# Eight buffers in place of six for one product, and a plan fitted to them: attention recurrence and gated MLP on one core

## The chip, the cores and the metric

The kernel runs on one core of a Trainium2 chip. Its engines are TensorE (PE, with its weight loads listed as PEld), VectorE (DVE), ScalarE (ACT), GpSimd (POOL) and SyncE (SP), which here issues all transfers. Each engine takes its instructions strictly in the order of the program. The metric is the device time of one execution in microseconds.

## The reference

A recurrent attention runs over 768 steps for 4 batches of 8 heads with head size 40, and its output goes through an MLP without an activation function:

```python
for t in range(S):
    y[:, :, t] = np.einsum('bhd,bhde->bhe', rt, state)
    Sa = np.einsum('bhde,bhe->bhd', state, at)
    state_decay = state * wt[:, :, None, :] - np.einsum('bhd,bhe->bhde', Sa, bt)
    state = state_decay + np.einsum('bhd,bhe->bhde', vt, kt)
...
x = np.ascontiguousarray(attn_out.transpose(0, 2, 1, 3)).reshape(B * S, H * D)
a = x @ w1
b = x @ w2
h = a * b @ w3
return (h @ w_out).astype(np.float32)
```

The MLP has 3072 tokens, 320 inputs and 1024 hidden columns. Its weights arrive as 64-bit numbers.

## The kernel before, in words

The 768 steps are cut into 12 chunks of 64. In a chunk the recurrence is a product with a triangular system, so that only 12 steps are sequential. A chunk is worked in four groups (g = 0 to 3, one for each batch, of four head pairs each). Its parts, with their lines:

- **load**: SP brings fm (decays and the k and b factors, L425) and al (a, L428).
- **scale**: DVE forms the running product of the decays (L438, L443), ACT its inverse (L447, L450), DVE refines that (L459, L463). lh is a times the decay (L455, POOL), and fm's second part is scaled by the inverse (L467).
- **causal**: PE multiplies lh with fm (L492). ACT copies parts of the result to JP and, negated, back into lh (both listed as L205), where POOL cuts the triangle (L510).
- **solve**: once a chunk, after the causal products of all four groups, DVE transposes JP (L524) and inverts the small triangular blocks in some fifty rows (L550, L554 and others up to L599 and L602). There is one buffer for this, ab.
- **join**: PE joins the inverted blocks (L625, L632), ACT copies them to TT.
- **pairs, tokens**: products that don't need the state (L669, L679, L694).
- **rec**: the recurrence of one group. PE reads the state (L719), multiplies with lh (L726), applies the solved blocks (L735); DVE masks the result (L740, four rows for a group); PE adds it up (L748); DVE forms the new state and the output y (L772, L792), PE transposes the state (L779). After L726 the group's lh is free, after L792 its fm.
- **gather, mlp**: SP moves y to xr (L802), ACT and DVE split it into two parts (L827, L830), PE multiplies (L844), ACT and DVE form the product of the two halves (L858, L861), PE multiplies by the product of w3 and w_out (L870), SP stores (L879).

In the head the weights are converted from 64 bits (L317 to L341) and split (L383, L395), and w3 is multiplied with w_out (L405). No MLP can begin before that.

What sets the order is a planner inside the kernel. Every operation is recorded with an engine, a cost, a due time, what it reads and writes, and the buffers it holds. `place()` then goes through a list schedule with these costs: on each engine the operation that can start first comes next, and among several the one with the earliest due time. A buffer of a pool is taken at the first operation that uses it and is given back after the last. The instructions are issued in that order, so the costs and the due times decide the program's order and nothing at run time. Numbers of buffers stand in `SLOTS`, distances of due times from a chunk's time in `P` (chunk time T0 + T x chunk), and `ON` says for some operations whether DVE or POOL does them in which chunk. lh is one pool of 6 buffers in the order of use, fm has 8, al 4.

Of the kernel before, what the change touches and what calls it, by code (L numbers as in the profile page):

```python
# [14 lines left out]
ALU = mybir.AluOpType  # L15
# [13 lines left out]
WMAX, GMIN = 1.5, 2.0 ** -40  # L29
CW = 512  # L30
LAT = dict(pe=0.33, act=0.09, dve=0.09, pool=0.1, sp=2.4, nil=0.0)
SLOTS = dict(rc=2, fm=8, al=4, lh=6, gi=2, gt=1, ab=1, TDX=1, rv=3, xu=3, bk=3, hs=2, st=2, y=1, xr=1, JP=2, TT=2, bank=6,
             raw=4, e=3, sg=3, mf=4, w3f=3, xs=1, gh=1, gl=1, ga=2, o=2)


ENGINES = tuple(getattr(mybir.EngineType, n) for n in ("PE", "Activation", "DVE", "Pool", "SP"))
T0, T = 32.93, 43.48
P = dict(w0=12.33, ws=3.58, ld=71.12, sc=40.48, ca=45.61, so=6.14, sp=45.27, jo=3.14, pa=8.34, tk=5.31, rg=14.14,
         ga=6.52, ml=90.63, kp=1.61, mt=25.46, mg=10.0)

ON = dict(cv="ppdpppdppppdddppppdpppppdddpppp", ws="d", lh="pppppppppppp", xs="dppppppppppp", gl="ppppppppppdd",
          cb="dddddddddddddddddddpdpddddddppp")


class Slot:


    def __init__(self, order, pool):
        self.order, self.pool, self.at, self.left, self.since, self.until = order, pool, None, 0, 0.0, 0.0
        if order.direct:  # L50
            self.at = order.turn[pool] = (order.turn.get(pool, -1) + 1) % SLOTS[pool]

# [5 lines left out]
class Order:  # L58
# [33 lines left out]
    def place(self):  # L92
# [3 lines left out]
        for o in ops:  # L96
            for d in o["deps"]:
                ops[d]["users"].append(o)
        free = {p: dict.fromkeys(range(n), 0.0) for p, n in SLOTS.items()}
        ready = {e: [] for e in LAT}  # L100
# [20 lines left out]

        uses = {p: {o["eng"] for o in ops for s in o["slots"] if s.pool == p} for p in SLOTS}
        placed, cand, spare = [], {}, {}

        def choice(e, starts):
            if not starts:
                return None
            first = min(t for t, _ in starts)
            return first, min((o for t, o in starts if t <= first + 1e-9),
                              key=lambda o: (o["due"] - P["kp"] * (e == "pe" and o["kind"] == last), o["n"]))  # L130

        while len(placed) < len(ops):
            best = None
            for e in LAT:
                if e not in cand:

                    starts, short = [], 1e9
                    for o in ready[e]:
# [3 lines left out]
                        elif e == "pe" and any(s.pool == "bank" and s.at is None for s in o["slots"]):  # L142
                            short = min(short, o["due"] + P["mg"])
                    some = [x for x in starts if x[1]["due"] < short or not any(s.at is None for s in x[1]["slots"])]
# [49 lines left out]
def attention_moe(ctx: ExitStack, tc: tile.TileContext, fmx, fma, rv, vt, sq, svr, w12, w12c, w3t, wo, out):  # L194
    nc = tc.nc
    pe, act, dve, pool = nc.tensor, nc.scalar, nc.vector, nc.gpsimd
    sp = nc.sync
# [10 lines left out]
    ident = cp.tile([128, 128], F32, name="ident")  # L208
# [3 lines left out]
    for q in range(2):  # L212
# [5 lines left out]
    pool.memset(first[:, :, 0:1], 1.0)  # L218
    parity = cp.tile([128, 1], F32, name="parity")

    dve.tensor_reduce(out=parity, in_=ident.rearrange("p (a b c) -> p a b c", a=4, b=2)[:, :, 1, :],
                      axis=mybir.AxisListType.XY, op=ALU.add)

    DG = cp.tile([128, 4, 8, 8], F32, name="DG")
    pool.memset(DG, 0.0)
# [11 lines left out]


    SB = cp.tile([104, NPC // 2, 2, 64], F32, name="SB")
    dve.memset(SB, 0.0)  # L240
    W3 = [cp.tile([128, NJ, DM], F32R, name=f"W3{n}") for n in "hl"]
    WT = [None] * 5
    for i in (0, 2):
# [4 lines left out]
    tiles = {}  # L248
    for name, shape in dict(fm=[104, 772], al=[104, NP, C], lh=[128, 2, NP, C], gi=[104, NP, C], gt=[104, NP, C], 
                            TDX=[128, 1024], rv=[104, 2, 2, 2 * C + D], xu=[128, 2, NP, C + D], bk=[128, NP, 104],  # L250
                            hs=[128, NP, C + D], st=[104, NP, D], y=[104, NP, TOK], xr=[128, 3, TOK],
                            JP=[128, NPC, 2, 32], TT=[128, NPC, C]).items():
        pl = cp if name == "TT" else ap_
        tiles[name] = [pl.tile(shape, F32, name=f"{name}{i}") for i in range(SLOTS[name])]
    for t in tiles["TT"]:
        dve.memset(t, 0.0)
    for t in tiles["al"]:
        dve.memset(t[32:64], 0.0)
    for t in tiles["rv"]:
        for h in range(2):  # L260
            q = slice(64 * h, 64 * h + 40)
            pool.tensor_copy(out=t[q].rearrange("q u x n -> q (u x) n")[:, :, 2 * C:],
                             in_=ident[q, q].unsqueeze(1).to_broadcast([40, 4, D]))
    tmp = ap_.tile([128, 1024], F32, name="tmp")
    R8 = ap_.tile([128, 8, 8], F32, name="R8")
    tiles["ab"] = [ps.tile([128, 1024], F32, name="ab")]
    tiles["bank"] = [ps.tile([128, 512], F32, name=f"bank{i}") for i in range(SLOTS["bank"])]


    cv, pp = ExitStack(), ExitStack()  # L270
    cvp = cv.enter_context(tc.tile_pool(name="cv", bufs=1, side="right"))
    for name, n, dt in (("raw", CW, I64), ("e", CW, U16), ("sg", CW, BF16), ("mf", CW, F32)):
        tiles[name] = [cvp.tile([128, n], dt, name=f"{name}{i}") for i in range(SLOTS[name])]
    ppp = pp.enter_context(tc.tile_pool(name="pp", bufs=1))
# [17 lines left out]
    op, slot = order.op, order.slot  # L292
# [16 lines left out]
    def convert(src, dst, due, w=()):  # L309
# [38 lines left out]
        op("dve", 0.62, due, f6, r=[raw], w=[mf], two=True)  # L348
        both(ON["cb"][k], 1.2, 0.38, due, f7, r=[e], w=[sg])
        both(ON["cv"][k], 1.25, 0.62, due, f8, r=[sg, "conv"], w=[mf] if dst is None else [mf, *w])  # L350
        return mf

    def weights():

        due, step = P["w0"], P["ws"]
        for k in range(3):
# [576 lines left out]
    for c in range(NCH):  # L933
        t0 = T0 + T * c
        jp_[c], tt_[c], y_[c] = slot("JP"), slot("TT"), slot("y")
        for g in range(B):
            load(c, g, t0 - P["ld"] + 2 * g)
        for g in range(B):
            scale(c, g, t0 - P["sc"] + 3 * g)
            causal(c, g, t0 - P["ca"] + 3 * g)  # L940
        solve(c, t0 - P["so"], P["sp"])
# [105 lines left out]
```

## Time and profile before

| what | us |
|---|---|
| median of three runs | 756.51 |
| the profiled execution, its own time | 756.74 |
| span of the profiled execution | 755.0 |
| busy PE, DVE, ACT, POOL | 608.8, 579.6, 480.3, 290.7 |
| first L844 (MLP) | 212.4 |
| last L870 ends | 749.1 |

The rows of the timeline have the start, the duration, the engine, the line and the operation, output and input, and in brackets the idle time before it with what ended it. In the rows of waits stand the waiting instruction, what it waited for, the sum, the number of times and the longest. In groups by line stand the busy time, the mean in ns, and the idle time before. Where a line's matmuls are listed, an f32 product counts two instructions.

### The profile page before, as it was taken

Reading aid. Unit: us, or ns where it says so; the run is one execution under the profiler, and the core shown is the slowest. Engines: PE = TensorE matmul, PEld = TensorE weight load, DVE = VectorE, ACT = ScalarE, POOL = GpSimd, SP = SyncE. Lnnn points to the kernel's source line nnn. Section 1 sums busy time; section 2 is a strip of 40 time slices with the busy share of each in tenths; the row PEclk is TensorE's granted clock in tenths of the full one; section 3 lists DMA queues with packets and bytes.
Section 4 is the critical chain, followed back from the end, with each engine's and each line's share of the span. In section 5 each row is a group of like instructions: output and inputs, shape, how many; then the busy total and the mean of one; then the engine's idle time right before and its main releaser. Section 6 shows DMA issues by size and latency. Waiting matters only on the chain.

```text
span 755.0 us, 23802 instructions
## 1 busy us (share of the span) xinstructions
PE 608.8 (81%) x9458; PEld 525.1 (70%) x9458; DVE 579.6 (77%) x1317; ACT 480.3 (64%) x1309; POOL 290.7 (39%) x374
## 2 busy tenths in 40 slices
PE   1312199658689899898898998998989989999996
PEld 1211176336579788797787887977878779788996
DVE  6969999899885895985968959859589498693421
ACT  3744466458857668768676687686767776836431
POOL 3155414534443363443533634435426244321000
PEclk9999999877779999999999999999999999999999
DMA  7833264134220312313113233142232231211010
GB/s 181 223 90 96 81 184 143 44 123 135 62 51 15 97 51 70 88 44 98 50 51 96 50 74 83 46 97 53 54 89 57 63 80 46 55 28 44 8 35 20
DMA packets 67554, 57.63 MB, mean 76 GB/s; under 512 B 31600, under 2 KB 58480, under 8 KB 67440
## 3 DMA queue, kind: packets, MB, share of 16 engines
q1 hardware_dynamic: 67440, 56.08, 27.9%
q8 instruction: 76, 1.25, 0.7%
q14 instruction: 38, 0.31, 0.1%
HBM read 47.40 MB, written 3.93 MB: 68 GB/s over the span
## 4 chain that ended last, share of the span: by engine, by line
DVE 31%; PE 21%; ACT 18%; issue 6%; SPq 3%; DMA 1%; POOL 0%; DVEq 0%; ACTq 0%; POOLq 0%
PE bank L844 8%; DVE tmp L550 6%; ACT JP L205 5%; ACT TT L205 4%; DVE xu L740 3%; PE bank L870 3%; PE bank L748 3%; SPq L802 3%; PE bank L492 2%; DVE ab L524 2%; DVE DG L554 2%; ACT xu L205 2%; DVE fm L443 2%; DVE ga L858 2%; DVE Tp L554 2%
## 5 line engine op out<-in xcount | busy, mean ns | idle before, releaser
L844 PE MATMUL bank<-xs,W 128*128 128x256 f32 x1536 | 205.5, 288 | 2.3 <-issue 1.7
L844 PEld LDWEIGHTS bank<-xs,W 128*128 128x128 f32 x1536 | 188.4, 190 | 10.3 <-issue 3.7
L740 DVE TENSOR_TENSOR xu<-bank,mask_h 64x208 f32<-64x208 f32 x192 | 71.2, 371 | 57.7 <-PE bank L735 54.5
L467 POOL TENSOR_TENSOR fm<-fm,gi 104x512 f32<-104x512 f32 x44 | 62.7, 1425 | 117.0 <-DVE gi L463 91.2
L205 ACT ACTIVATE xu<-bank 64x128 f32<-64x128 f32 (+2 forms) x368 | 90.7, 297 | 19.0 <-PE bank L669 9.2
L205 ACT ACTIVATE JP<-bank 32x256 f32<-32x256 f32 (+1 forms) x216 | 75.7, 350 | 38.2 <-PE bank L492 34.8
L510 POOL TENSOR_SCALAR_AFFINE_SELECT lh<-lh 64x256 f32<-64x256 f32 x96 | 39.9, 415 | 129.6 <-ACT lh L205 125.8
L455 POOL TENSOR_TENSOR lh<-al,fm 104x512 f32<-104x512 f32 x48 | 59.5, 1245 | 43.5 <-PE bank L726 32.5
L748 PE MATMUL bank<-xu,bk 128*40 128x104 f32 (+1 forms) x768 | 49.6, 262 | 24.2 <-DVE xu L740 24.2
L726 PE MATMUL bank<-xu,lh 104*64 104x104 f32 (+2 forms) x768 | 53.2, 272 | 17.4 <-ACT xu L205 9.1
L861 POOL TENSOR_TENSOR gl<-ga,gh 128x512 fp32r<-128x512 f32 x40 | 51.5, 1286 | 32.8 <-ACT gh L205 32.8
L679 POOL TENSOR_SCALAR_AFFINE_SELECT xu<-xu 64x256 f32<-64x256 f32 x96 | 41.2, 429 | 57.7 <-ACT xu L205 49.6
L870 PE MATMUL bank<-W3h,gh 128*128 128x320 f32 x192 | 63.2, 329 | 0.0
L748 PEld LDWEIGHTS bank<-xu,bk 128*40 128x40 f32 (+1 forms) x768 | 37.4, 118 | 34.0 <-DVE xu L740 29.0
L726 PEld LDWEIGHTS bank<-xu,lh 128*64 128x64 f32 (+2 forms) x768 | 41.4, 145 | 27.9 <-ACT xu L205 16.5
L870 PE MATMUL bank<-W3l,gh 128*128 128x320 f32 x192 | 59.3, 309 | 0.0
L870 PE MATMUL bank<-W3h,gl 128*128 128x320 f32 x192 | 59.1, 308 | 0.0
L205 ACT ACTIVATE gh<-ga 128x512 fp32r<-128x512 f32 x48 | 30.1, 628 | 38.1 <-DVE ga L858 37.8
L447 ACT ACTIVATE gi<-fm 104x256 f32<-104x256 f32 x48 | 20.0, 416 | 53.7 <-DVE fm L443 51.2
L694 PE MATMUL bank<-ident,fm 104*128 104x104 f32 x192 | 28.8, 277 | 29.9 <-DMA al<-in_fma_dram 11.6
L405 PE MATMUL bank<-wof,w3f 128*128 128x320 f32 x128 | 44.2, 497 | 6.4 <-POOL w3f L341 6.2
L492 PE MATMUL bank<-lh,fm 40*64 40x64 f32 x1536 | 38.8, 238 | 12.8 <-POOL fm L467 8.3
(102 smaller groups left out, 1297.5 us busy)
## 6 DMA issues: line engine op xcount, KB each, us to landing
fm<-in_fmx_dram SPq DMA_DIRECT2D x48, 313.6 KB
raw<-in_w3t_dram SPq DMA_DIRECT2D x16, 512.0 KB
rv<-in_rv_dram SPq DMA_DIRECT2D x96, 80.0 KB
raw<-in_w_dram SPq DMA_DIRECT2D x8, 512.0 KB
al<-in_fma_dram SPq DMA_DIRECT2D x96, 40.0 KB
xu<-in_vt_dram SPq DMA_DIRECT2D x96, 40.0 KB
out_dram<-o SPq DMA_DIRECT2D x48, 80.0 KB
xr<-y SPq DMA_DIRECT2D x72, 40.0 KB
```

Of the source, the lines that this page charges most:

```text
L205: act.activation(out_, in_, AF.Copy, scale=scale)
L405: pe.matmul(out=pt.t[:, 0:DM], lhsT=w[:, j], rhs=wof[:, j], start=(j == 0), stop=(j == NJ - 1))
L455: e.tensor_tensor(out=lh.t[0:104], in0=al.t.unsqueeze(1).to_broadcast(full), in1=gam(c, g)[:, :, 0:C].unsqueeze(1).to_broadcast(full), op= ...
L467: e.tensor_tensor(out=X, in0=X, in1=gi.t.unsqueeze(2).to_broadcast([104, NP, 2, C]), op=ALU.mult)
L492: pe.matmul(out=bank(ab)[64 * x:64 * x + 64, p], lhsT=X[r, p, x], rhs=lh.t[r, ab, p], start=True, stop=True)
L550: dve.tensor_tensor(out=scratch(*shape), in0=x().to_broadcast([128, *shape]), in1=y().to_broadcast([128, *shape]), op=ALU.mult)
L726: pe.matmul(out=view(hp)[64 * ab:64 * ab + 64, p], lhsT=lh.t[k, ab, p], rhs=xu.t[k, ab, p], start=True, stop=True)
L740: dve.tensor_tensor(out=xu.t[64 * ab:64 * ab + 64, ab, k:NP:2], in0=qs[ab].t[r, 256:256 + 2 * N].rearrange("p (n t) -> p n t", n=2), in1=m ...
L748: pe.matmul(out=q(r, p), lhsT=bk.t[:, p, r], rhs=xu.t[:, ab, p], start=(c == 0), stop=True, skip_group_check=True)
L844: pe.matmul(out=pt.t[:, TOK * x:TOK * x + TOK], lhsT=WT[k][:, cs], rhs=xs.t[:, z], start=(n == 0), stop=(n == 7))
L861: both(ON["gl"][c % NCH], 1.35, 0.62, t + 1, lambda e, a=a, j=j: e.tensor_tensor(out=gl.t[:, j:j + 2], in0=a.t, in1=gh.t[:, j:j + 2], op=A ...
L870: pe.matmul(out=pt.t[:, 0:DM], lhsT=l.t[:, j, ts], rhs=W3[r][:, j], start=(j == 0 and n == 0), stop=(j == NJ - 1 and n == 2))
```

## The change

lh gets eight buffers, al three. The numbers in `P` are new, and with them the due times. In `ON` a few operations change between DVE and POOL: L467 of chunk 8 goes to DVE, L861 of chunks 7 and 10 to DVE and that of chunk 11 to POOL, two L338 to DVE and one L341 to POOL. At the start the memsets change their order, al first.

```diff
-SLOTS = dict(rc=2, fm=8, al=4, lh=6, gi=2, gt=1, ab=1, TDX=1, rv=3, xu=3, bk=3, hs=2, st=2, y=1, xr=1, JP=2, TT=2, bank=6,
+SLOTS = dict(rc=2, fm=8, al=3, lh=8, gi=2, gt=1, ab=1, TDX=1, rv=3, xu=3, bk=3, hs=2, st=2, y=1, xr=1, JP=2, TT=2, bank=6,
...
-P = dict(w0=12.33, ws=3.58, ld=71.12, sc=40.48, ca=45.61, so=6.14, sp=45.27, jo=3.14, pa=8.34, tk=5.31, rg=14.14,
-         ga=6.52, ml=90.63, kp=1.61, mt=25.46, mg=10.0)
-
-ON = dict(cv="ppdpppdppppdddppppdpppppdddpppp", ws="d", lh="pppppppppppp", xs="dppppppppppp", gl="ppppppppppdd",
-          cb="dddddddddddddddddddpdpddddddppp")
+P = dict(w0=13.15, ws=3.46, ld=92.51, sc=40.41, ca=51.28, so=6.14, sp=36.96, jo=5.76, pa=9.53, tk=2.89, rg=10.82,
+         ga=5.8, ml=85.76, kp=3.48, mt=30.46, mg=11.62)
+
+ON = dict(cv="ppdpppdppppdddppppdpppppddppppp", ws="d", lh="pppppppppppp", xs="dpppppppdppp", gl="pppppppdppdp",
+          cb="dddddddddddddddddddpdpddddddddp")
...
-    dve.tensor_reduce(out=parity, in_=ident.rearrange("p (a b c) -> p a b c", a=4, b=2)[:, :, 1, :],
-                      axis=mybir.AxisListType.XY, op=ALU.add)
...
-    dve.memset(SB, 0.0)
...
-    for t in tiles["TT"]:
-        dve.memset(t, 0.0)
-    for t in tiles["al"]:
-        dve.memset(t[32:64], 0.0)
...
+    for t in tiles["al"]:
+        dve.memset(t[32:64], 0.0)
+    dve.memset(SB, 0.0)
+    for t in tiles["TT"]:
+        dve.memset(t, 0.0)
+    dve.tensor_reduce(out=parity, in_=ident.rearrange("p (a b c) -> p a b c", a=4, b=2)[:, :, 1, :],
+                      axis=mybir.AxisListType.XY, op=ALU.add)
```

Most of what the change does is in the order that the planner makes of this. Three places of it follow.

DVE, from the end of a chunk's solve (L602) on, before. Names: TDX the solved blocks, xs the MLP's input, fm the decays, xu the masked rows:

```order
L602 STREAM_TRANSPOSE TDX_117<-TDX_117 128x512
L830 TENSOR_TENSOR xs_1852<-xr_132,xs_1852 128x768
L438 TENSOR_SCALAR fm_103,stats<-fm_103 104x260
L443 SCALAR_TENSOR_TENSOR fm_103<-fm_103,first 104x260
L459 TENSOR_TENSOR gt_116<-fm_103,gi_115 104x256
L463 SCALAR_TENSOR_TENSOR gi_115<-gt_116,gi_115 104x256
L740 TENSOR_TENSOR xu_122<-bank_154,mask_h 64x2x104
```

The same place now, in every second chunk of the repeating part:

```order
L602 STREAM_TRANSPOSE TDX_116<-TDX_116 128x512
L443 SCALAR_TENSOR_TENSOR fm_101<-fm_101,first 104x260
L459 TENSOR_TENSOR gt_115<-fm_101,gi_114 104x256
L463 SCALAR_TENSOR_TENSOR gi_114<-gt_115,gi_114 104x256
L858 TENSOR_TENSOR ga_1864<-bank_153,ga_1864 128x512
L524 STREAM_TRANSPOSE ab<-JP_133 128x1024
L550 TENSOR_TENSOR tmp<-DG,ab 128x4
L554 TENSOR_REDUCE DG<-tmp 128x4
L550 TENSOR_TENSOR tmp<-DG,ab 128x16
```

The next chunk's solve (L524) now begins ahead of this chunk's masks (L740); thirteen solve rows of L550 and L554 and one L830 stand between L524 and the masks. Before, L524 stood behind the masks and outputs of two groups. In the other chunks it now follows the masks of the first group.

DVE, from a group's output to the next use of the same fm buffer, before:

```order
L792 TENSOR_TENSOR y_131<-bank_153,fm_98 104x2x64
L792 TENSOR_TENSOR y_131<-bank_157,fm_98 104x2x64
L554 TENSOR_REDUCE ab<-tmp 128x8x4
L858 TENSOR_TENSOR ga_1853<-bank_155,ga_1853 128x512
L459 TENSOR_TENSOR gt_116<-fm_97,gi_115 104x256
L463 SCALAR_TENSOR_TENSOR gi_115<-gt_116,gi_115 104x256
L550 TENSOR_TENSOR tmp<-Tp,ab 128x256
```

There follow three more solve rows and four masks, and then L438 of fm_98. The shortest such stretch now:

```order
L792 TENSOR_TENSOR y_130<-bank_157,fm_97 104x2x64
L792 TENSOR_TENSOR y_130<-bank_154,fm_97 104x2x64
L594 TENSOR_TENSOR ab<-R_150,ab 128x8x8
L550 TENSOR_TENSOR tmp<-ab,DG 128x512
L554 TENSOR_REDUCE Tp<-tmp 128x8x8
L599 STREAM_TRANSPOSE TDX_116<-Tp 128x32x16
L602 STREAM_TRANSPOSE TDX_116<-TDX_116 128x512
L438 TENSOR_SCALAR fm_97,stats<-fm_97 104x260
```

Between giving the buffer back and wanting it filled again stand five rows of DVE; the load lies between them, on SP.

PE, between the recurrences of two groups, from the sum (L748) of the first group of a chunk on. lh is read by L726. Now:

```order
L748 MATMUL bank_153<-xu_121,bk_124 40x104 x4
L748 MATMUL bank_154<-xu_121,bk_124 40x104 x4
L726 MATMUL bank_155<-xu_122,lh_106 64x104 x8
L694 MATMUL bank_156<-ident,fm_97 128x104 x4
L779 MATMUL bank_153<-ident,st_128 40x104 x4
L844 MATMUL bank_154<-xs_1862,W_0_91 128x256 x2
```

Before, the same place reads:

```order
L735 MATMUL bank_154<-hs_128,TT_136 64x104
L735 MATMUL bank_152<-hs_128,TT_136 64x104
L748 MATMUL bank_153<-xu_121,bk_124 40x104 x4
L748 MATMUL bank_157<-xu_121,bk_124 40x104 x4
L694 MATMUL bank_155<-ident,fm_103 128x104 x4
```

Before, the first two groups of a chunk went together, L735 of both ahead of L748 of the first. Now in the repeating part the first group's L748 comes before the second group's L735, with MLP rows (L870, L844) between them.

## The prediction, as put on record

> **What bounds the kernel now.** I read the page first, then the windows, then the timeline of one repeating stretch, engine by engine.
>
> ```profile
> span 755.0 us, 23802 instructions
> PE 608.8 (81%) x9458; PEld 525.1 (70%) x9458; DVE 579.6 (77%) x1317; ACT 480.3 (64%) x1309; POOL 290.7 (39%) x374
> PE   1312199658689899898898998998989989999996
> DVE  6969999899885895985968959859589498693421
> ```
>
> The rows by slices show two regimes: a head of some eleven slices in which DVE is full and PE is not, and a body in which PE is at 8 or 9 of 10 and DVE swings. The windows (columns: PE, PEld, DVE, ACT, POOL busy us, then clock and DMA) put numbers on them.
>
> ```profile
> 0.00:213.50 213.50, 108.69 (x1469) 80.38 (x1469) 190.13 (x393) 124.45 (x312) 87.10 (x116) 0.91 0.42 121
> 245.50:295.40 49.90, 46.03 (x786) 40.25 (x784) 39.49 (x96) 36.22 (x104) 22.48 (x29) 1.00 0.27 70
> 497.30:547.20 49.90, 46.09 (x785) 40.36 (x786) 39.47 (x96) 36.21 (x104) 22.02 (x29) 1.00 0.28 70
> 693.50:755.00 61.50, 55.00 (x568) 52.21 (x566) 20.44 (x44) 17.45 (x38) 0.82 (x2) 0.99 0.09 23
> ```
>
> The body repeats chunk by chunk. Its first and last chunk begin (first L735 of chunk 2 and of chunk 11) at:
>
> ```profile
> 245.49 0.59 PE L735 MATMUL bank<-hs,TT 64*64 64x104 f32 x16
> 693.46 1.27 PE L735 MATMUL bank<-hs,TT 64*64 64x104 f32 x32
> ```
>
> That is nine intervals of (693.46 - 245.49)/9 = 49.8 us. No engine is full in them: PE is busy 46.1, DVE 39.5. So a cycle of waits sets the interval. DVE's timeline shows it:
>
> ```profile
> 497.28 3.12 DVE L740 TENSOR_TENSOR xu<-bank,mask_h 64x208 f32<-64x208 f32 x8 [5.00 <-PE bank L735]
> 503.21 1.98 DVE L524 STREAM_TRANSPOSE ab<-JP 128x1024 f32<-128x1024 f32 x1 [1.31 <-ACT JP L205]
> 512.72 1.53 DVE L740 TENSOR_TENSOR xu<-bank,mask_h 64x208 f32<-64x208 f32 x4
> 520.26 1.53 DVE L740 TENSOR_TENSOR xu<-bank,mask_h 64x208 f32<-64x208 f32 x4
> 530.24 0.68 DVE L550 TENSOR_TENSOR tmp<-ab,DG 128x512 f32<-128x512 f32 x1
> 536.48 0.71 DVE L602 STREAM_TRANSPOSE TDX<-TDX 128x512 f32<-128x512 f32 x1
> 541.28 0.42 DVE L459 TENSOR_TENSOR gt<-fm,gi 104x256 f32<-104x256 f32 x1 [2.17 <-ACT gi L450]
> 547.23 1.95 DVE L740 TENSOR_TENSOR xu<-bank,mask_h 64x208 f32<-64x208 f32 x5 [5.00 <-PE bank L735]
> ```
>
> DVE masks two head groups (L740), starts the solve (L524), works without a pause to the solve's end (L602 ends at 537.2), and then has next to nothing until PE has joined the blocks and reached the next chunk's L735: a handoff of 10.0 us (537.2 to 547.2), idle in 7.2 of it. With the 1.31 before L524 that is 8.5 idle, so DVE is occupied 49.9 - 8.5 = 41.4 us a chunk. PE's side of the same stretch:
>
> ```profile
> 510.23 2.15 PE L844 MATMUL bank<-xs,W 128*128 128x256 f32 x16
> 513.91 1.13 PE L748 MATMUL bank<-xu,bk 128*40 128x104 f32 x16 [1.52 <-DVE xu L740]
> 514.97 1.21 PE L844 MATMUL bank<-xs,W 128*128 128x256 f32 x8
> 516.71 0.54 PE L779 MATMUL bank<-ident,st 104*40 104x104 f32 x4 [0.53 <-DVE y L792]
> 525.32 6.83 PE L844 MATMUL bank<-xs,W 128*128 128x256 f32 x56
> 537.46 1.20 PE L625 MATMUL bank<-TDX,JP 32*32 32x32 f32 x64
> 540.55 1.20 PE L632 MATMUL bank<-TDX,JP 32*32 32x32 f32 x64
> 542.75 0.94 PE L719 MATMUL bank<-rv,SB 40*64 40x104 f32 x32
> 546.52 0.59 PE L735 MATMUL bank<-hs,TT 64*64 64x104 f32 x16
> ```
>
> PE loses time where DVE is late with a mask (1.52) or with the new state (0.53). What holds the cycle closed is lh. Six buffers are a chunk and a half, so the last two groups of the next chunk can be scaled only when L726 of this chunk has read its lh; the waits say so:
>
> ```profile
> POOL lh L455 <- PE bank L726: 32.5, 18, 6.4
> PE bank L748 <- DVE xu L740: 24.2, 23, 4.2
> ```
>
> **The change part by part.** *Eight lh.* All four causal products of a chunk can now stand before the recurrence of the chunk ahead, so L524 no longer waits for them. In the new DVE order the next solve's L524 and thirteen further rows stand inside the handoff in every second chunk; in the others L524 follows the first mask directly. In the first kind the handoff's 7.2 us of idle time is filled by L524 (1.98) and the small solve rows (503.21 to 509.36 in this trace, 6.2 with L524). The 1.31 before L524 goes in both.
>
> To price it I add up both engines' new rows over two chunks, with t = 0 at the first L735. Durations are those of the timeline, a mask set 1.53, a solve row of 512 elements 0.68, L625 1.13 to the next row; L844 and L870 come from the end of the chain, where PE has nothing else:
>
> ```profile
> 726.85 15.24 PE bank L844 x128
> 742.09 7.06 PE bank L870 x48
> ```
>
> That is 0.95 for eight L844 and 0.88 for six L870, each some 0.2 more where another kind stands before it (514.97 to 516.18 for eight). The same addition over the old order gives 50.0, against 49.9 shown. First chunk: masks of the four groups start at 0.7, 8.9, 16.7 and 23.5, where PE has their L735 done at 0.4, 7.8, 14.9 and 22.1; solve rows stand in DVE's way by about 1 to 2 us each time. The last state is ready at 27.7. PE then runs 32 rows of L844, L625, 16, L632, 16 and the first products, and is at the next L735 at 44.0; DVE, done with its solve near 32, idles in this handoff. Second chunk: masks at 44.7, 55.8, 59.0 (in two halves) and 70.1, L735 done at 44.4, 53.8, 56.1 and 68.5; last state at 74.6, the solve ends at 83.7, PE reaches L625 at 84.3 and the next L735 at 95.4, while DVE has L524 and its rows to do. So 95.4 for two chunks, 47.7 for one: 2.1 less than 49.8. PE still loses some 3 us a chunk, since the masks are later behind solve rows than PE is.
>
> Bounds of the interval: not under DVE's occupied 41.4, nor under PE's busy time with its named waits gone, about 45; above, the old 49.8 and more if a new wait comes (below).
>
> *Three al in place of four.* al is read by L455 alone on POOL, which is busy 22 of 49.9 us; a buffer fewer lets its load start one group later. Covered by POOL's idle time; without that cover L455 would be late by one load, about 3.6 us (next row), for the fourth group. I take 0.
>
> *fm stays at eight.* fm is given back by L792 and wanted again by L438 of the chunk after next. Issue to use is, at the start of this trace, 8.83 - 5.25 = 3.6 us:
>
> ```profile
> 4.24 1.09 DVE L258 MEMSET al<- 32x256 f32 x4
> 4.54 0.67 SPq L428 DMA_DIRECT2D al<-in_fma_dram  x2
> 5.25 0.33 SPq L425 DMA_DIRECT2D fm<-in_fmx_dram  x1
> 8.83 0.42 DVE L438 TENSOR_SCALAR_CACHE_REDUCE fm<-fm 104x260 f32<-104x260 f32 x1 [2.17 <-DMA fm<-in_fmx_dram]
> 516.38 0.48 DVE L792 TENSOR_TENSOR y<-bank,fm 104x128 f32<-104x128 f32 x2
> 516.88 0.31 SPq L425 DMA_DIRECT2D fm<-in_fmx_dram  x1
> 521.83 0.42 DVE L438 TENSOR_SCALAR_CACHE_REDUCE fm<-fm 104x260 f32<-104x260 f32 x1
> ```
>
> In the old order the tightest group has 521.83 - 516.86 = 5.0 us of DVE rows between the two, the others up to 14; in the new one, by the same durations, nearly all have 3.5 to 5.7. So DVE will wait here now and then. Between 0 and 4 x 0.5 us a chunk; I take 0.5, as most stay above 3.6.
>
> *The start.* Memsets of al now come first, so SP's first al load (held to 4.54 by L258) and the second fm move up by some 3 us; DVE's wait of 2.17 shrinks. Against it stand seven more DVE rows ahead of the first L830 (376 to 383): two L338 and two L792, five solve rows, less an L341 and a memset, near 3 us. Between -4 and +3; I take -1.5.
>
> *Due times, and what they move.* The rows of PE ahead of the first L844 are the same in number and kind. Behind the last L748, 11 groups of eight L844 stand in place of 7, about 4 us of PE work (32 x 15.24/128) moved out of the body, where it filled gaps, to the end, where PE has none. If the body were PE-bound this would cost nothing, if DVE-bound 4; I take +2. L467 of one chunk goes to DVE, and two L338; one L341 goes to POOL; L861 moves between chunks.
>
> ```profile
> L467 DVE TENSOR_TENSOR fm<-fm,gi 104x512 f32<-104x512 f32 x4 | 2.8, 692 | 0.1
> ```
>
> That is 2.8 us on DVE in one interval, nothing if it falls into DVE's idle handoff; I count it in the +2.
>
> *Sum.* 9 x (49.8 - 47.7 - 0.5) = -14.4; start -1.5; end +2. Together -13.9 on the span of 755.0: 741.1. The profiled run took 756.74, 1.7 more than its span, and the median is 756.51, so about 742.5; I say 742.
>
> **The rivals.** *The handoffs vanish altogether* (chance 0.11). If PE loses nothing to late masks, only DVE's idle time counts: 17.0 per two chunks, less 2.6 and 6.8, leaves 7.6, and the interval is (82.8 + 7.6)/2 = 45.2. That is 9 x 4.6 = 41 less, some 716. For it: PE's waits are short and many. Against it: DVE would be 92% occupied, in fixed order. [...]
>
> *One stall for another* (0.15). The solve rows ahead of the masks cost PE what the handoff saves; the interval stays within 0.3 of 49.8, the time at 753 to 759. For it: mask sets start 1 to 2 us after PE's L735 in six of eight places. Against it: the addition above counts that already.
>
> *The reload decides* (0.12). SP works in order, and fm's load stands behind out and xr rows. With SP free 2 us late, each of four L438 a chunk waits about 1.3 us, DVE's 41.4 becomes 46.6 and all its masks shift: 47.7 + 5 = 52.7, 9 x 2.9 = 26 more, about 782. It decides from about 0.5 us of wait per reload on. For it: the margin falls from 5 to about 4. Against it: in the old body no L438 waits at all. [...]
>
> **How the numbers follow.** My forecast has 0.62, with 734 to 751 as its own range (an interval of 46.8 to 48.7). Eight in ten: 727 to 758, which leaves out most of the first rival and the last. What can be told from no change here is 0.5%, 3.8 us. Faster: 0.61 + 0.11 and a little of the second rival, 0.73; same 0.15; slower 0.12.
>
> **What would show it.** Right: first L735 of every second chunk 94 to 98 us apart; DVE's wait for L735 down from twelve long ones (54.5 us) to about half; L455 hardly waiting for L726; L779 and L748 still waiting for DVE, L779 more than now. Wrong: L438 waiting for fm by more than 2 us a chunk (the third rival), intervals of equal length near 49.8 (the second), or a PE row without gaps near 45 (the first).

## The result: 1.1% faster, about half of what was forecast

| | before | changed |
|---|---|---|
| median, us | 756.76 | 748.93 (747.29 to 750.51) |
| ratio to before, 95% interval | | 0.9886, 0.9854 to 0.9919 |
| profiled execution, its span | 756.74, 755.0 | 749.88, 748.1 |
| first L844 | 212.39 | 212.66 |
| first L735 of chunk 2, of chunk 11 | 245.49, 693.46 | 242.76, 679.08 |
| last L870 ends | 749.1 | 741.8 |

The forecast was 742, so 7.8 us came where 14.5 were expected. Of the runs further down, one execution of e1 (831.8 us) and one of e6 (762.7) fell into a slower state and are left out of the ratios. First the page of the changed kernel (span, busy times, and from the rows by slices PE, DVE and the granted clock of PE):

```profile
span 748.1 us, 23793 instructions
PE 606.7 (81%) x9458; PEld 523.9 (70%) x9458; DVE 583.0 (78%) x1321; ACT 482.1 (64%) x1309; POOL 288.9 (39%) x369
PE   2320299578669899998999998999989999999996
DVE  8979989998996985969949879599688796962420
PEclk9999999758669999999999999999989999999999
```

The busy times have hardly moved: of the 6.9 us by which the span fell, 4.8 are time in which PE had nothing to do. The one 8 in the second half of the clock's row is new (the granted clock is 0.82 in the mean from 542.3 to 561.1), and will matter below. The windows, now cut at the first L735 of chunk 2 and of chunk 11 (columns as in the prediction), first of the kernel before:

```profile
245.50:693.50 448.00, 413.74 (x6998) 362.83 (x6996) 348.17 (x846) 318.53 (x912) 188.51 (x242) 1.00 0.26 65
693.50:755.00 61.50, 55.00 (x568) 52.21 (x566) 20.44 (x44) 17.45 (x38) 0.82 (x2) 0.99 0.09 23
```

and of the changed one:

```profile
242.80:679.10 436.30, 406.78 (x6926) 358.01 (x6926) 347.63 (x848) 315.56 (x900) 172.59 (x229) 0.99 0.26 66
679.10:748.10 69.00, 62.77 (x618) 59.31 (x618) 18.54 (x41) 19.73 (x43) 6.79 (x7) 0.98 0.10 24
```

These four rows and the start are the whole account. The body is 11.7 shorter and the end 7.5 longer. PE's busy time in both together is the same (468.7 and 469.6), but the end has 7.8 more of it and the body 7.0 less. So most of the body's gain is work that was only put off; PE's idle time fell from 34.3 to 29.5, by 4.8, in the body, and by 0.3 in the end. With 2.7 from the start that is the 6.9 of the span, less 0.9 by which PE was busy longer.

The waits of the changed kernel, the rows that answer to those of the prediction:

```profile
PE bank L779 <- DVE y L792: 13.2, 15, 1.2
PE bank L748 <- DVE xu L740: 9.6, 8, 3.4
DVE xu L740 <- PE bank L735: 20.5, 9, 7.7
DVE fm L438 <- DMA fm<-in_fmx_dram: 3.0, 6, 0.9
DVE ga L858 <- PE bank L844: 39.4, 12, 7.3
```

L455 no longer waits for L726 in any row of the list. DVE's wait for L735 (54.5 before) is down to 20.5, L748's (24.2) to 9.6, and L779 waits more than it did (5.7). But DVE's idle time moved more than it fell. In the body alone its wait for L735 went from 45.4 to 5.4 us, and its idle time in all only from 99.8 to 88.7: it now waits at L858, the product of the MLP's two halves, for PE (the last row, 19.7 before) and for ACT.

### The profile page after: what moved, and what is told of

Same layout as the page of the kernel before. It is cut to its first block, busy times and chain, and to the rows that moved or that the text cites. A ratio compares the mean times of both kernels' runs of the same rounds, so it can differ in the third digit from the quotient of the medians.

```text
span 748.1 us, 23793 instructions
## 1 busy us (share of the span) xinstructions
PE 606.7 (81%) x9458; PEld 523.9 (70%) x9458; DVE 583.0 (78%) x1321; ACT 482.1 (64%) x1309; POOL 288.9 (39%) x369
## 4 chain that ended last, share of the span: by engine, by line
DVE 47%; PE 36%; ACT 9%; issue 4%; DMA 2%; POOL 1%; SPq 0%; DVEq 0%; POOLq 0%; ACTq 0%
PE bank L844 14%; PE bank L870 7%; DVE tmp L550 6%; DVE xu L740 5%; DVE mf L334 4%; PE bank L726 3%; ACT JP L205 3%; DVE ab L524 2%; DVE gi L463 2%; DVE ab L554 2%; PE bank L735 2%; ACT TT L205 2%; DVE Tp L554 2%; PE bank L748 2%; DVE DG L554 2%
## 5 line engine op out<-in xcount | busy, mean ns | idle before, releaser
L844 PE MATMUL bank<-xs,W 128*128 128x256 f32 x1536 | 208.3, 289 | 9.5 <-issue 6.2
L844 PEld LDWEIGHTS bank<-xs,W 128*128 128x128 f32 x1536 | 190.2, 192 | 18.3 <-issue 7.7
L205 ACT ACTIVATE xu<-bank 64x128 f32<-64x128 f32 (+2 forms) x368 | 92.5, 297 | 41.8 <-PE bank L719 27.9
L455 POOL TENSOR_TENSOR lh<-al,fm 104x512 f32<-104x512 f32 x48 | 59.4, 1237 | 126.1 <-DVE fm L443 53.7
L740 DVE TENSOR_TENSOR xu<-bank,mask_h 64x208 f32<-64x208 f32 x192 | 71.2, 371 | 23.6 <-PE bank L735 20.5
L861 POOL TENSOR_TENSOR gl<-ga,gh 128x512 fp32r<-128x512 f32 x40 | 51.9, 1297 | 73.7 <-ACT gh L205 70.8
L858 DVE TENSOR_TENSOR ga<-bank,ga 128x512 f32<-128x512 f32 x48 | 32.9, 686 | 57.0 <-PE bank L844 39.4
L467 POOL TENSOR_TENSOR fm<-fm,gi 104x512 f32<-104x512 f32 x40 | 56.6, 1415 | 47.4 <-DVE gi L463 46.4
L870 PE MATMUL bank<-W3h,gh 128*128 128x320 f32 x192 | 64.2, 335 | 0.6 <-ACT ga L205 0.6
L726 PE MATMUL bank<-xu,lh 104*64 104x104 f32 (+2 forms) x768 | 50.1, 273 | 15.7 <-POOL xu L679 8.8
L870 PE MATMUL bank<-W3l,gh 128*128 128x320 f32 x192 | 59.7, 311 | 0.0
L870 PE MATMUL bank<-W3h,gl 128*128 128x320 f32 x192 | 59.7, 311 | 0.0
L726 PEld LDWEIGHTS bank<-xu,lh 104*64 104x64 f32 (+2 forms) x768 | 40.4, 147 | 22.9 <-POOL xu L679 9.1
L748 PE MATMUL bank<-xu,bk 128*40 128x104 f32 (+1 forms) x768 | 47.7, 265 | 9.8 <-DVE xu L740 9.6
L205 ACT ACTIVATE gh<-ga 128x512 fp32r<-128x512 f32 x48 | 30.1, 626 | 37.3 <-DVE ga L858 37.2
L748 PEld LDWEIGHTS bank<-xu,bk 128*40 128x40 f32 (+1 forms) x768 | 36.4, 121 | 18.4 <-DVE xu L740 12.5
L492 PE MATMUL bank<-lh,fm 40*64 40x64 f32 x1536 | 35.9, 237 | 15.3 <-POOL fm L467 11.1
L492 PEld LDWEIGHTS bank<-lh,fm 40*64 40x64 f32 x1536 | 29.4, 146 | 23.8 <-POOL fm L467 13.0
```

Of the source, the lines that this page charges most:

```text
L205: act.activation(out_, in_, AF.Copy, scale=scale)
L455: e.tensor_tensor(out=lh.t[0:104], in0=al.t.unsqueeze(1).to_broadcast(full), in1=gam(c, g)[:, :, 0:C].unsqueeze(1).to_broadcast(full), op= ...
L467: e.tensor_tensor(out=X, in0=X, in1=gi.t.unsqueeze(2).to_broadcast([104, NP, 2, C]), op=ALU.mult)
L492: pe.matmul(out=bank(ab)[64 * x:64 * x + 64, p], lhsT=X[r, p, x], rhs=lh.t[r, ab, p], start=True, stop=True)
L726: pe.matmul(out=view(hp)[64 * ab:64 * ab + 64, p], lhsT=lh.t[k, ab, p], rhs=xu.t[k, ab, p], start=True, stop=True)
L740: dve.tensor_tensor(out=xu.t[64 * ab:64 * ab + 64, ab, k:NP:2], in0=qs[ab].t[r, 256:256 + 2 * N].rearrange("p (n t) -> p n t", n=2), in1=m ...
```

## The experiments

Theory A of the first four runs was the prediction's: eight buffers close the handoff, the due times cost a little at the end, the memsets give 1 to 3 us. The rival of each stands in its expectation. All times in one table, each ratio against runs of the kernel before on the same chip; "low clock" is the time after 230 us and before the last chunk's tail in which the granted clock was 0.5, summed from windows of 0.25 us.

| run | median us | ratio to before, 95% | first L735, chunk 2 and 11 | low clock, us |
|---|---|---|---|---|
| before | 756.8 | | 245.5, 693.5 | 0 |
| the change | 748.9 | 0.9886 (0.9854 to 0.9919) | 242.8, 679.1 | 10.2 |
| e1, lh and al alone | 772.1 | 1.0178 (1.0135 to 1.0220) | 255.2, 709.1 | 22.2 |
| e2, all but lh and al | 771.1 | 1.0182 (1.0151 to 1.0214) | 243.8, 707.9 | 68.1 |
| e3, memsets alone | 754.8 | 0.9973 (0.9959 to 0.9987) | 243.9, 691.6 | 0 |
| e4, ml=60 | 805.6 | 1.0644 (1.0611 to 1.0678) | 248.9, 727.4 | 95.7 |
| e5, e2 with products added | 772.2 | 1.0206 (1.0184 to 1.0227) | 243.4, 709.0 | 30.6 |
| e6, the change with products added | 755.5 | 0.9974 (0.9959 to 0.9989) | 242.8, 684.1 | 6.8 |
| e7, the change again | 750.5 | 0.9923 (0.9896 to 0.9949) | 245.4, 679.4 | 6.8 |
| e8, ml=80 | 763.2 | 1.0076 (1.0060 to 1.0092) | 243.9, 702.0 | 30.6 |
| e9, nine fm, other due times | 752.6 | 0.9943 (0.9920 to 0.9966) | 248.5, 678.3 | 23.8 |
| e10, other due times | 744.3 | 0.9836 (0.9814 to 0.9858) | 245.2, 676.7 | 6.8 |
| e11, old due time of the loads | 766.7 | 1.0123 (1.0100 to 1.0146) | 244.6, 703.2 | 44.3 |
| e12, four al | 747.8 | 0.9877 (0.9855 to 0.9899) | 243.7, 678.9 | 10.2 |

### e1: the buffers alone

```diff
-... al=4, lh=6 ...      (the kernel before)
+... al=3, lh=8 ...
```

> The kernel before with eight lh and three al alone; its due times, its choice of engines and its start stay. Theory A (the gain comes from the eight buffers: the solve's L524 can start inside the handoff or right behind the first mask): the interval between chunks falls from 49.8 to 47.7-48.8 us, the work behind the last chunk's first L735 stays that of before, time 745 to 751. Rival B (the gain comes from the new due times, which space the four groups): intervals near 49.8, time 755 to 758.

772.1: slower by 1.8%, which neither theory had. Of the 15.4 us on the span, 9.7 lie ahead of chunk 2 and 5.9 in the nine intervals, now 50.4 in the mean. For the intervals the waits of DVE name one cause, the reload, which the prediction had as a rival for the whole change:

```profile
DVE fm L438 <- DMA fm<-in_fmx_dram: 26.8, 9, 5.6
```

It was 3.3 before; 23.6 of the 26.8 lie behind the first L735 of chunk 2. SP's and DVE's timeline of this run shows how it comes about:

```profile
333.00 8.96 SPq L802 DMA_DIRECT2D xr<-y  x12
342.01 0.55 SPq L425 DMA_DIRECT2D fm<-in_fmx_dram  x1
346.50 0.42 DVE L438 TENSOR_SCALAR_CACHE_REDUCE fm<-fm 104x260 f32<-104x260 f32 x1 [4.71 <-DMA fm<-in_fmx_dram]
```

The load of fm stands behind the twelve moves to xr, and these take 9 us. In the changed kernel it stands ahead of them:

```profile
319.62 0.32 SPq L425 DMA_DIRECT2D fm<-in_fmx_dram  x1
319.99 10.83 SPq L802 DMA_DIRECT2D xr<-y  x12
```

e11 looks at this again. The larger part of the loss is the longer head (first L844 at 225.9, 13.5 later); no run took that apart.

### e2: everything but the buffers

```diff
-... al=3, lh=8 ...      (the changed kernel)
+... al=4, lh=6 ...
```

> The changed kernel with six lh and four al: new due times, new choice of engines, new start. Theory A: L524 stands behind two mask sets again, intervals near 49.8, time 752 to 757 (less than before only by what the start gives). Rival B: 747 to 751.

771.1: as bad as the other half alone. In the planned order of this kernel no MLP row is left between L625, L632 and L726 in chunks 3 to 10 (between L625 and L719 the kernel before has 2.7 us of them there, the change 2.7 to 5.3, at 0.95 and 0.88 a group), and on DVE only L830 stands in the handoff. The timelines of PE and of DVE:

```profile
336.41 1.20 PE L625 MATMUL bank<-TDX,JP 32*32 32x32 f32 x64
338.98 0.24 PE L632 MATMUL bank<-TDX,JP 32*32 32x32 f32 x2 [1.37 <-ACT JP L205]
347.12 3.12 DVE L740 TENSOR_TENSOR xu<-bank,mask_h 64x208 f32<-64x208 f32 x8 [10.26 <-PE bank L735]
```

and DVE's wait over the whole span, 54.5 before:

```profile
DVE xu L740 <- PE bank L735: 103.1, 13, 10.6
```

The interval is 51.2 to 51.4 in the first four chunks. At the same time the clock is at 0.5 for 6.8 us or more ahead of the first L735 of each of the chunks 2 to 10, inside that bare handoff: in the one shown from 339.2 to 346.1. Which of the two is the cause, e5 asks.

### e3: the memsets alone

```diff
+    for t in tiles["al"]:
+        dve.memset(t[32:64], 0.0)
     dve.memset(SB, 0.0)
     for t in tiles["TT"]:
         dve.memset(t, 0.0)
-    for t in tiles["al"]:
-        dve.memset(t[32:64], 0.0)
```

> The kernel before with the memsets at the start in the new order alone. If the earlier first loads are passed on through the head, first L735 of chunk 2 comes 1 to 3 us earlier and the time is 753.5 to 755.5; if DVE's full head swallows them, 756 to 757.

754.8, a ratio of 0.9973, and the first L735 of chunk 2 comes 1.6 us earlier, with intervals of 49.8 as before. The memsets are worth about 2 us of the 7.8.

### e4: the MLP due earlier

```diff
-         ga=5.8, ml=85.76, ...     (the changed kernel)
+         ga=5.8, ml=60.0, ...
```

> The changed kernel with the MLP's due times 25.76 us earlier (ml 60 in place of 85.76). Behind the last L748 stand 16 groups of L844 and 10 of L870 in place of 27 and 16, some 16 us less. Theory: PE's work is the same in all, so only idle time counts, and the time stays within 3 us of the changed kernel's 748.9. Rival (the backlog behind the recurrence is what ate the gain): 5 to 8 us less, 741 to 744.

805.6, outside all that was expected. Eleven of the 27 groups of L844 behind the last L748 moved ahead of it, as meant, but in the body PE's rows themselves are longer. A handoff of this run:

```profile
344.26 1.60 PE L625 MATMUL bank<-TDX,JP 32*32 32x32 f32 x64 [3.28 <-ACT lh L205]
347.20 1.91 PE L632 MATMUL bank<-TDX,JP 32*32 32x32 f32 x62 [0.30 <-ACT JP L205]
349.04 2.31 PE L719 MATMUL bank<-rv,SB 40*64 40x104 f32 x32
```

L625 took 1.20 elsewhere and L719 0.94 in the kernel before. Over the body the granted clock is 0.90 in the mean:

```profile
248.90:727.40 478.50, 439.98 (x6921) 387.45 (x6920) 351.41 (x850) 311.10 (x896) 173.40 (x228) 0.90 0.23 60
```

Its order has no MLP row in the handoffs of chunks 4 to 7, 9 and 10 and almost none in that of 3, and a low stretch begins near each of these seven handoffs and near no other.

### e5 and e6: products added where PE waits

```diff
+    def warm(pt, n):
+        for i in range(n): pe.matmul(out=pt.t[:, 0:TOK], lhsT=WT[0][:, 0:128], rhs=WT[0][:, TOK:2 * TOK], start=True, stop=True)
...
-        op("pe", 1.15, due + 3, f2, ...
+        op("pe", 1.15, due + 3, lambda: (warm(p2, 16 if c > 1 else 0), f2()), ...
```

In e6 the same stands ahead of L779, six products in eleven groups, and eight ahead of L632 of chunk 10.

> The changed kernel with lh=6 and al=4 again (771.1 us), and now with 16 extra products of 128x256 (the instruction of L844) ahead of L632 in chunks 2 to 11, written to the bank that L632 then overwrites: 16 x 0.12 = 1.9 us of TensorE work a chunk, where TensorE waits 1.4 + 0.4 us for JP and has no MLP row. Nothing else moves. Theory A, the granted clock: with six buffers nothing of the MLP stands between L625, L632 and L726 in chunks 3 to 10, a stretch of 3.4 us then counts as idle and the next 6.8 us run at half clock, in the middle of the handoff. With the extra products the low stretches of the body go (low clock after 205 us from 81 us in all to under 25), each handoff is 2 to 3 us shorter, and the time is 742 to 757 although work was added. Theory B, the handoff itself is late (DVE's L602, ACT's copies) and the clock only shows it: the time stays at 771 to 775.

772.2, no faster than e2, though the low clock fell from 68 to 31 us (theory A had it all but go). DVE's wait is what it was:

```profile
DVE xu L740 <- PE bank L735: 105.0, 13, 12.3
```

The number is theory B's, but the run doesn't part the two. The steps that theory A speaks of are in e2's trace: ahead of the low stretches of chunks 3 to 10 PE was busy 1.2 to 2.0 of 3.41 us, and half clock followed for 6.8 us, once for 13.7; that such a step counts as idle was my reading and is not shown. The products stand in the path that they speed up: from L625 to L735 it took 10.0 us in e2 and 9.4 here, with 1.9 us of work more. And at the price that e7 gives below, 0.4 us for one, the 68 us of low clock in e2 would be worth some 27, more than the 14 that it lost. A third reading is open too: in both runs many of the low stretches begin 51.2 us apart, which is 15 of the steps of 3.41 us in which the clock changes (last section), and the intervals are about as long. Whether these steps hold the interval there, no run tests. So what makes e2 slow, the bare handoff or the clock in it, stays open.

> The changed kernel with 6 extra products of 128x256 (0.7 us) ahead of L779 in eleven groups where TensorE waits 0.9 to 1.2 us for L792 anyway, and 8 ahead of L632 of chunk 10; they are overwritten. Theory A: the two low stretches of the body (6.8 us at 550, 3.4 us at 629) go or get shorter, the intervals of chunks 8 and 9 fall from 51.9 and 53.1 to 47 to 51, and the time is 743 to 747. Theory B: the extra work lengthens every group it stands in, by up to 0.3 us each, and the time is 749 to 753.

755.5, above theory B. The products did not fall into the wait. They need a bank (one of the six buffers that take PE's results), and wait for L792, which is still reading one:

```profile
PE bank L414 <- DVE y L792: 11.6, 11, 1.2
```

```profile
348.57 0.98 PE L414 MATMUL bank<-W 128*128 128x256 f32 x6 [1.01 <-DVE y L792]
349.39 0.52 PE L779 MATMUL bank<-ident,st 104*40 104x104 f32 x4
```

(first the waits, then PE's timeline; L414 is the added product). So 0.8 us was added eleven times on the path, and 5 of these 9 us came out at the end, against e7 beside it. The run tells nothing on the clock, but it corrects a reading: the added products don't use the state at all and wait as long as L779 did, so that row is most likely a wait for the bank, with the state ready at about the same time.

### e7: the changed kernel a second time

> The changed kernel itself, a second time and on the same chip as its neighbours: 747 to 750.5. If low stretches come from windows of the clock that run freely against the program, they lie at other places than 550 and 629 in its profile, and chunk 8 without one takes about 47 in place of 51.9. If they belong to the order of the rows, they lie at the same places.

750.5, and a price for the clock. In the first profile the clock is low at 550.3 (6.8 us) and 628.8 (3.4), in the second at 454.2 (6.8) alone. So the places don't belong to the order of the rows alone. The same rows in both, around L779 of chunk 8, in windows of 3.4 us; the first profile:

```profile
546.80:550.20 3.40, 1.89 (x36) 1.33 (x36) 3.29 (x11) 2.10 (x8) 0.43 (x1) 1.00 0.24 61
550.30:553.70 3.40, 3.40 (x39) 2.69 (x38) 3.26 (x6) 2.06 (x7) 1.99 (x4) 0.50 0.46 134
553.70:557.10 3.40, 3.40 (x31) 2.67 (x33) 2.41 (x8) 0.93 (x3) 1.57 (x3) 0.50 0.01 2
```

and the second, where the rows come 3.8 us later:

```profile
550.30:553.70 3.40, 2.18 (x38) 1.62 (x36) 3.28 (x11) 2.09 (x9) 0.11 (x1) 1.00 0.20 61
553.70:557.10 3.40, 3.11 (x59) 2.48 (x60) 3.26 (x8) 3.04 (x12) 1.98 (x4) 1.00 0.60 146
```

The interval from chunk 8 to 9 is 51.9 with the low stretch and 49.2 without, that from chunk 9 to 10 is 53.1 and 51.7, that from chunk 6 to 7, where only the second profile has one, 46.5 and 49.0. So 6.8 us at half clock cost 2.5 to 2.7, and 3.4 cost 1.4: 0.4 us for one, from two executions. The change's profile lost about 4 us that way. Chunk 8 was expected to take about 47 without it; it takes 49.2, and what the other 2 us are, no run shows.

### e8: less left for the end

```diff
-         ga=5.8, ml=85.76, ...     (the changed kernel)
+         ga=5.8, ml=80.0, ...
```

> The changed kernel with the due time of the MLP at 80 in place of 85.76 from the chunk's time. In its order no handoff from chunk 2 to 11 is without MLP rows, and behind the last L748 there are 23 groups of eight L844 in place of 27. Theory A (the end was mis-sized because work was left for it): 4 groups less at 0.95 us, so 743 to 747, with at most two low stretches of the clock. Theory B (the work taken out of the end is paid in the body, which has no room for it): 748 to 752.

763.2, worse than theory B. The two windows of this run:

```profile
243.90:702.00 458.10, 423.85 (x6978) 373.59 (x6978) 354.45 (x847) 315.84 (x905) 178.30 (x229) 0.97 0.25 64
702.00:762.80 60.80, 55.08 (x568) 52.21 (x566) 17.68 (x40) 17.41 (x38) 5.99 (x6) 0.98 0.10 23
```

The end is back at 60.8, 8.2 shorter than the change's, and the body is 21.8 longer. PE is idle 34.3 there, as before the change, and busy 17 more, 7.7 of it the work brought back; the other 9 go with 30.6 us at half clock. A due time that takes work out of the end moves the waits of the whole body with it.

### e9 and e10: other due times, with nine fm and with eight

```diff
-P = dict(w0=13.15, ws=3.46, ld=92.51, sc=40.41, ca=51.28, so=6.14, sp=36.96, jo=5.76, pa=9.53, tk=2.89, rg=10.82,
-         ga=5.8, ml=85.76, kp=3.48, mt=30.46, mg=11.62)
+P = dict(w0=12.23, ws=3.56, ld=70.15, sc=43.87, ca=45.3, so=5.32, sp=39.69, jo=12.64, pa=5.63,
+         tk=3.71, rg=14.28, ga=9.53, ml=87.99, kp=3.0, mt=22.07, mg=12.22)       (e9, with fm=9)
+P = dict(w0=13.12, ws=3.53, ld=108.78, sc=39.52, ca=43.93, so=6.73, sp=42.07, jo=4.92, pa=6.59,
+         tk=1.98, rg=11.01, ga=0.46, ml=88.84, kp=2.99, mt=29.97, mg=12.87)      (e10, with fm=8)
```

> The changed kernel with nine fm in place of eight and another set of due times, found by laying the planned rows out with the durations and the delays between engines that the traces so far show (that reckoning gives the spans of the kernel before, of the change without its low stretches of the clock, and of the runs with six buffers and with the old due times within 2 to 8 us). Theory A: after the change the interval is still set by waits between engines, not by a full engine, so a ninth fm and due times that use it shorten it again, to about 46 us: the reckoning gives a span of 725, with up to 10 us for low stretches of the clock 727 to 737. Theory B: TensorE at about 45 of 48.5 us a chunk and its clock are the bound now, so nothing more comes out of the order: 744 to 752.

752.6, just above theory B. Its intervals are 47.8 in the mean, 0.7 less than the change's. But its start is 5.7 longer, and 4.0 us more work than in the change (66.75 of PE against 62.77) lie in its end, from 678.3 on. DVE now waits elsewhere. ACT's and DVE's timeline in a handoff, and a window of it:

```profile
374.87 2.55 ACT L205 ACTIVATE TT<-TDX 32x512 f32<-32x512 f32 x4 [2.13 <-DVE TDX L599]
379.93 2.55 ACT L205 ACTIVATE JP<-bank 32x512 f32<-32x512 f32 x6
384.91 1.32 ACT L205 ACTIVATE JP<-bank 32x256 f32<-32x256 f32 x4
386.26 2.01 DVE L524 STREAM_TRANSPOSE ab<-JP 128x1024 f32<-128x1024 f32 x1 [5.66 <-ACT JP L205]
```

```profile
374.90:386.30 11.40, 10.34 (x258) 9.26 (x256) 3.56 (x11) 11.03 (x27) 6.08 (x6) 1.00 0.18 43
```

ACT is busy 11.03 of 11.40 us there. Once the next solve stands in the handoff, ACT's row of copies (TT, JP, lh, gh, TT, JP) is what L524 waits for, 42.3 us in all between 240 and 690. My reckoning for this run was 26 us too short; how much of that is ACT's copies and how much the 23.8 us of low clock stays open.

> The changed kernel with its own eight fm, and only other due times found in the same way. Theory A: the reckoning gives a span of 734, with the clock 735 to 745; the difference from the run with nine fm is then the worth of the ninth buffer, some 8 us. Theory B: as good as the changed kernel or worse, 747 to 755.

744.3, theory A, and faster than both kernels: the changed buffers with other due times give 0.9836 (0.9814 to 0.9858). Its two windows:

```profile
245.20:676.70 431.50, 406.77 (x6948) 360.40 (x6948) 347.92 (x846) 315.30 (x905) 175.56 (x228) 0.99 0.26 67
676.70:741.10 64.40, 58.39 (x592) 55.48 (x590) 17.94 (x40) 18.03 (x39) 5.99 (x6) 0.97 0.10 25
```

PE's work in the body is that of the change, its idle time 24.7 in place of 29.5, and the end has 4.4 less work. The change with four al (e12), run beside it on the same chip, took 747.8. What the ninth fm is worth these two runs don't tell, since their due times differ.

### e11: the loads' due time put back

```diff
-... ld=92.51 ...      (the changed kernel)
+... ld=71.12 ...
```

> The changed kernel with one number put back: fm and al are due 71.12 us ahead of their chunk, as before, in place of 92.51. Theory A (with eight lh the load must be issued earlier: SP does it in order, and with the old due time it comes behind the twelve moves to xr that take 9 us, as in the run with eight lh alone, where DVE waited 23.6 us for fm): L438 waits for fm by 5 us or more in all, and the time is 753 to 760. Theory B (the load's due time is a detail): 747 to 752, L438 waits under 3 us.

766.7, worse than theory A's range, and in its direction:

```profile
DVE fm L438 <- DMA fm<-in_fmx_dram: 13.4, 8, 3.8
```

against 3.0 in the change. The waits alone are 10 us; 44 us at half clock (10 in the change) come with them, at 0.4 us each another 14 or so. The two overlap, and the run doesn't part them. Nor does one number change the loads alone: the planner's whole order follows it, and behind the first L735 of chunk 11 stand 17 groups of six L870 here, where the change has 24.

### e12: al

```diff
-... al=3 ...      (the changed kernel)
+... al=4 ...
```

> The changed kernel with four al in place of three. My term for this was 0, since L455 on POOL has room: 747 to 751, no difference that can be measured. Rival: three al delay L455 by a load of 3.6 us now and then, and with four the time is 742 to 746.

747.8, a ratio of 0.9877 against 0.9886 for the change: no difference. The term 0 stands.

## Why the prediction was right, and where it was wrong

The direction and the range held, and of the mechanism the part that fills the handoff: in the body DVE's wait for L735 all but went (45.4 to 5.4 us). How the time came together was another than forecast, and that the sum still came near is in part luck.

**The step that failed first is the end**, "11 groups of eight L844 stand in place of 7 ... I take +2". It measured +7.5. I had counted L844 behind the last L748 (27 groups now and 23 before; 11 and 7 leave out the last 16, which are in both), and priced the four groups between nothing and 4 us. But the border between body and end is the first L735 of chunk 11, since that is where the nine intervals stop. Behind it stand 32 groups of L844 in both kernels: none was moved out of the body. What was moved is L870: 24 of its 96 groups of six are left there, against 16 before. The last rows of the change's chain give their price; the last row is eight such groups:

```profile
712.61 7.04 PE bank L870 x48
719.65 15.06 PE bank L844 x128
734.71 7.06 PE bank L870 x48
```

Nothing hides there, so 7.06 was to be had from the same rows that the prediction quoted. And it is not a cost beside the body's gain but a part of it: the last interval is 37.3 us, because its work was put off.

**Body**, predicted -14.4, measured -11.7. The two are near only by luck, since three things make up the -11.7:

| from the first L735 of chunk | before | changed | difference |
|---|---|---|---|
| 2 to 8, six intervals | 301.0 | 294.0 | -7.1 |
| 8 to 10, two intervals | 101.0 | 105.0 | +4.0 |
| 10 to 11, the last interval | 46.0 | 37.3 | -8.6 |

The first L735 of chunk 8 and of chunk 10, before and then changed (those of chunks 2 and 11 stand in the table of the result):

```profile
546.52 0.59 PE L735 MATMUL bank<-hs,TT 64*64 64x104 f32 x16
647.50 0.59 PE L735 MATMUL bank<-hs,TT 64*64 64x104 f32 x16
536.73 0.59 PE L735 MATMUL bank<-hs,TT 64*64 64x104 f32 x16
641.75 0.59 PE L735 MATMUL bank<-hs,TT 64*64 64x104 f32 x16 [0.62 <-ACT hs L205]
```

The six are what the prediction was about: 1.2 us an interval, where it had 1.6 with the reload in it. The two hold the low clock, and are no shorter than before without it (100.9 in e7). The last is the work put off. Without these 7 us the nine intervals gained some 4.6, and 8.6 with the 4 us of low clock taken off as well. Over the first eight the mean is 49.9 (49.5 in e7), against 50.3 before.

The pairing came as added up: intervals of 46.2, 51.4, 47.2, 51.3, 46.5, 51.4, in pairs 97.6, 98.5 and 97.9, where the sign was 94 to 98; the next pair is 105.0. The chunk with the solve inside takes 51.4, to the tenth what the addition gave (95.4 - 44.0). The other was to take 44.0 and takes 46.5. PE's rows of chunk 6, where that chunk starts at 438.82, show where:

```profile
467.41 0.54 PE L779 MATMUL bank<-ident,st 104*40 104x104 f32 x4 [0.45 <-DVE y L792]
469.20 4.04 PE L844 MATMUL bank<-xs,W 128*128 128x256 f32 x32 [0.90 <-ACT SB L205]
473.18 1.20 PE L625 MATMUL bank<-TDX,JP 32*32 32x32 f32 x64
485.34 0.54 PE L735 MATMUL bank<-hs,TT 64*64 64x104 f32 x16
```

L779 starts 28.6 after the first L735 where I had the last state at 27.7, then PE waits 0.90 for ACT's copy of the state, which I had at nothing, and L625 follows at 34.4, not at 31.5. From there to L735 it is 12.2, and I had 12.5. So of the 2.9 us a third was lost in the groups ahead, a third is the wait for ACT, and the rest is L779 and other rows of PE in between. L844 doesn't read the state; that it waits for the bank which this copy empties is likely and not shown.

**Low clock**, not foreseen at all: 10.2 us in the body where the kernel before has none, some 4 us of time.

**The start** was priced -1.5 and gave -2.7; the memsets alone gave -1.6 at the same place (e3). The second profile of the change (e7) has only -0.1 there, so this term is known no better than to some 3 us.

**The reload in the change**, priced 0.5 a chunk, 4.5 in all: 3.0 in all, the longest 0.9. The rival built on it had a mechanism that other kernels show: with the old due time of the loads DVE waits 23.6 us for fm behind the first L735 of chunk 2 in e1, and 13.4 in all in e11, which is a part of what these two lost. What keeps it small is `ld`, which I had passed over among the due times.

**lh, L748, L779, L735, al**: as forecast, the lh wait gone, L748's down to 40%, L779's up, DVE's wait for L735 down to 38%, al worth nothing.

**The other rivals.** That the handoffs vanish did not happen (some 716 us); one stall for another came nearer than its 0.15: the pairs at full clock are 1 to 2 us under 2 x 49.8, but DVE's idle time in the body fell by 11.1 where its wait for L735 fell by 40. What I had not seen is that neither half of the change would be faster alone: buffers and due times each cost 2% without the other.

The sum by what was measured: -2.7 (start) - 11.7 (body, with 4 of low clock in it) + 7.5 (end) = -6.9 on the span, against -13.9.

## What to carry to other kernels

When an order is planned, price moved work by what lies on each side of the same border at which the intervals are counted, for every kind of row, and take the busy time of the bounding engine on both sides first: if it only moves, nothing is gained. A buffer count and the due times that use it are one change, so neither can be judged by a run of the other alone; the queue that issues the reload is the first place to look (in e1 the load of fm stood behind twelve moves that took 9 us). On PE, leave some dense rows in every stretch of some 3 us: in these profiles a step of 3.41 us in which PE was busy less than 1.7 was each time followed by at least 3.4 us at a granted clock of 0.5.

## What the runs showed of the hardware that was not expected

The granted clock falls to 0.50 inside a busy body, without any long pause of PE. In the profile of the change PE is idle 0.35 and 1.15 us around 547 to 550, and busy 1.89 of the 3.40 us ahead of the drop. In the bodies the low stretches last 3.4 us (the change, at 628.8), 6.8 (the change, at 550.3), 10.2 (e9, at 578.9), 13.7 (e4, at 344.8), 17.1 (e4, at 614.5) or 20.5 (e11, from 388.6 to 409.1), and within one profile they begin on a grid of 3.41 us (628.8 and 744.9 in the change lie 23 and 57 such steps behind 550.3). Cut along that grid, eleven profiles (before, the change, e1, e2, e4, e5, e7 to e10 and e12) show for the steps at full clock between some 240 and 690 us: where PE was busy less than 1.7 of 3.41 us, in 13 steps, half clock followed each time; where it was busy more than 2.6, in 1213, never; of the 126 in between, 28 were followed by it. A step that is itself at half clock can be busy throughout and still be followed by another (550.30 to 553.70 in the rows of e7). Where the grid falls against the rows differs from execution to execution: in e7 the rows around chunk 8 come 3.8 us later than in the first profile, and the steps begin 0.5 us earlier (549.8 for 550.3), so the same order has such a stretch in one chunk now and in another then.
